# The second layer of batches one and two as seven block products, in a written order

## The chip, the cores and the metric

One core of a Trainium2 chip runs the whole program. The metric is the device time of one execution in microseconds; it is told as the median of the runs. Data lies in HBM; tiles of 128 partitions lie in SBUF; TensorE multiplies from SBUF into PSUM banks; VectorE, ScalarE and GpSimd work on the tiles; SyncE issues all DMA here.

## What is computed

```
scores = scale * q @ k.T               # batch 4, heads 12, seq 448, head_dim 64
scores = where(causal mask, -1e9, scores - max)
attn   = exp(scores) / sum
x      = (attn @ v) as [1792 tokens, 768]
gate   = 1 / (1 + exp(-(x @ w_gate)))  # w_gate, w_val: 768 x 1536
out    = (gate * (x @ w_val)) @ w_out  # w_out: 1536 x 768
```

All inputs are float32. The weights come as 64-bit words and are turned into float32 on the chip.

## The kernel before

Everything is kept transposed: features lie on partitions, the 448 tokens of a batch on the free axis. A float32 product is made of three products of a reduced type, fp32r: each operand is split into a high part (a ScalarE cast) and a low part (the operand minus its high part, on VectorE or GpSimd), and TensorE adds high x high, high x low and low x high into one bank. Such a triple is one operation of the plan, with the cost 0.608. One product has 128 x 128 weights and 448 columns.

Attention runs over 24 pairs of heads, six to a batch. For a pair: `load`, `wscore` (TensorE, line 394), `softmax` (line 417 on VectorE, 424 on ScalarE, scaling on GpSimd at line 445), `shift` (a transpose by VectorE, line 460, and a trip of the tile to DRAM and back, `pd`, `pt`), `wpv` (TensorE, line 488), `features`. The first six pairs take another path (`score`, `trans`, `pv`).

The perceptron runs in units. `unit_items(0)` and `unit_items(1)` handle batches one and two singly. The first layer (`f_in`) has 12 blocks jj, each with a gate and a value group of six triples over k; line 622 takes the gate, line 628 the gated product, lines 630 and 631 split it. The second layer (`f_out`) has six output blocks m of 12 triples each. `weight(p)` gets the weights of a group: for unit 0 it loads 64-bit words into a part of the tile `room` (768 KB), makes float32 of them (lines 570, 572, 574), keeps a copy in DRAM (`wdram`, line 577) and splits (lines 582, 584); for unit 1 it fetches the copy. Batches three and four are handled together by `pair_items` (line 814 on TensorE): each layer as seven products of half-size blocks with sums of blocks before and after, instead of eight. `pair_inputs` makes its sums and parts of the inputs, `mix` sums of weights, `out_inputs` those of the second layer's inputs.

The order is made in two steps. The bottom of the kernel lists all operations with due times: the units' triples in sequence, the attention steps of batches two to four spread over them by a pacing line (`TURN`, `SPREAD`). Then `Plan.order` simulates the engines with costs and due times (with hand-given shifts, `NUDGE`) and gives out the instructions in that order; each engine, and SyncE's DMA queue, works through its own list in order. Tiles of one tag share a ring of `BUFS[tag]` buffers, so an operation that writes a new tile waits for the users of the tile that many places back. `lock=True` marks VectorE operations that the simulation keeps apart from GpSimd's.

## Time and profile before

| what | value |
|---|---|
| median of 3 runs | 620.17 us (619.71 to 620.87) |
| span of the profiled execution | 617.8 us (the page lists no other time for it) |
| instructions | 11857 |
| TensorE busy | 606.7 us, 98% |
| VectorE, ScalarE, GpSimd busy | 442.5, 334.0, 306.3 us |
| DMA | 153.35 MB, mean 248 GB/s |

Busy time of an engine counts overlapping instructions once. The mean of a group is the length of one instruction by itself, with its overlap. The stages of the span: opening to some 40 us, first layer of batch one to 152.7, its second layer to 221, batch two to 382, batches three and four after that.

### The profile page before, as it was taken

What the parts mean: (1) busy time and instruction counts of PE and PEld (TensorE: products, weight loads), DVE (VectorE), ACT (ScalarE), POOL (GpSimd) and SP (SyncE); (2) the same over time, 40 slices, a digit from 0 to 9 for tenths busy, and PEclk for the clock granted to TensorE, in tenths of its full rate; (3) what the DMA queues carried; (4) which work ended last, traced back from release to release, by engine and by line L of the source; (5) the groups of instructions that cost most, each with busy time, mean ns of one, the idle gap of its engine ahead of it and who ended that gap; (6) DMA issues with size and microseconds to landing.
All of it is one profiled execution on the core that took longest, in us unless ns stands there. A gap on an engine that the chain in (4) does not pass through costs nothing.

```text
span 617.8 us, 11857 instructions
## 1 busy us (share of the span) xinstructions
PE 606.7 (98%) x4182; PEld 532.1 (86%) x4182; DVE 442.5 (72%) x1048; ACT 334.0 (54%) x754; POOL 306.3 (50%) x350
## 2 busy tenths in 40 slices
PE   6999999999989999999999999999999999999997
PEld 4578888898988888888888899999999989999996
DVE  5988999888856555455558856588746469999852
ACT  7997666666445655554657645443343443556420
POOL 4750434441300775877757766666746665501200
PEclk9999999999999999999999999999999999999999
DMA  8699999999999999888877896765433213534321
GB/s 292 198 305 343 367 375 384 319 407 364 349 380 337 360 333 335 285 305 288 298 276 254 291 324 222 271 230 178 153 103 103 77 53 102 161 119 149 104 76 59
DMA packets 54492, 153.35 MB, mean 248 GB/s; under 512 B 6048, under 2 KB 12704, under 8 KB 52128
## 3 DMA queue, kind: packets, MB, share of 16 engines
q1 hardware_dynamic: 54432, 152.59, 70.1%
q8 instruction: 33, 0.54, 0.3%
q14 instruction: 27, 0.22, 0.1%
HBM read 109.31 MB, written 43.25 MB: 247 GB/s over the span
## 4 chain that ended last, share of the span: by engine, by line
PE 89%; DMA 5%; DVE 3%; issue 1%; POOL 0%; ACT 0%; SPq 0%; DVEq 0%; ACTq 0%
PE m L601 38%; PE m L814 20%; PE s L814 11%; PE t L814 7%; PE m L488 5%; PE s L394 4%; PE t L394 2%; DMA room<-in_wp_dram 2%; DMA pd<-tb 1%; DVE sm L417 1%; PE t L320 1%; DMA wdram<-wr 1%; DMA vr<-in_vt_dram 1%; DVE pt L331 1%; PE m L344 0%
## 5 line engine op out<-in xcount | busy, mean ns | idle before, releaser
L768 POOL TENSOR_TENSOR wl<-room,wh 128x384 fp32r<-128x384 f32 x84 | 97.9, 1188 | 56.9 <-ACT wh L767 54.3
L445 POOL TENSOR_SCALAR sm<-sm,r 128x128 f32<-128x128 f32 (+3 forms) x165 | 91.1, 575 | 60.1 <-DVE r L435 37.6
L601 PE MATMUL m<-xh,wh 128*128 128x448 f32 x288 | 107.2, 372 | 0.0
L601 PE MATMUL m<-xh,wl 128*128 128x448 f32 x288 | 105.3, 366 | 0.0
L601 PE MATMUL m<-xl,wh 128*128 128x448 f32 x288 | 105.3, 365 | 0.0
L424 ACT ACTIVATE sm<-sm,mn 128x128 f32<-128x128 f32 (+3 forms) x168 | 87.7, 526 | 12.9 <-DVE mn L417 12.1
L584 POOL TENSOR_TENSOR wl<-wr,wh 128x768 fp32r<-128x768 f32 x38 | 70.8, 1880 | 29.4 <-ACT wh L582 29.3
L582 ACT CAST wh<-wr 128x768 fp32r<-128x768 f32 x72 | 59.4, 830 | 30.6 <-DVE wr L574 14.4
L767 ACT CAST wh<-room 128x384 fp32r<-128x384 f32 x84 | 39.7, 511 | 60.3 <-PE s L814 19.0
L601 PEld LDWEIGHTS m<-xh,wh 128*128 128x128 f32 x288 | 54.1, 188 | 6.5 <-issue 1.3
L601 PEld LDWEIGHTS m<-xh,wl 128*128 128x128 f32 x288 | 54.1, 188 | 4.5
L601 PEld LDWEIGHTS m<-xl,wh 128*128 128x128 f32 x288 | 54.1, 188 | 4.2
L417 DVE CUSTOM_DVE_ANT_0 sm<-s,mask 128x128 f32<-128x128 f32 (+3 forms) x108 | 42.7, 408 | 17.2 <-PE s L394 17.0
L601 PE MATMUL m<-gh,wh 128*128 128x448 f32 x144 | 53.3, 370 | 0.0
L601 PE MATMUL m<-gh,wl 128*128 128x448 f32 x144 | 52.6, 365 | 0.0
L601 PE MATMUL m<-gl,wh 128*128 128x448 f32 x144 | 52.6, 365 | 0.0
L631 POOL TENSOR_TENSOR gl<-gt,gh 128x448 fp32r<-128x448 f32 x24 | 29.0, 1212 | 41.6 <-ACT gh L630 41.6
L814 PE MATMUL m<-pt,wh 128*128 128x448 f32 x150 | 44.7, 366 | 0.0
L460 DVE STREAM_TRANSPOSE room<-sm 128x384 f32<-128x384 f32 (+2 forms) x84 | 36.0, 452 | 9.3 <-POOL sm L445 8.7
L394 PE MATMUL s<-raw 64*64 64x128 f32 (+3 forms) x432 | 36.9, 392 | 4.3 <-DMA raw<-in_qkt_dram 2.9
L584 DVE TENSOR_TENSOR wl<-wr,wh 128x768 fp32r<-128x768 f32 x34 | 33.4, 981 | 10.5 <-ACT wh L582 10.4
L488 PEld LDWEIGHTS m<-pt,vr 128*64 128x64 f32 x720 | 33.5, 137 | 7.8 <-issue 6.5
(177 smaller groups left out, 1378.3 us busy)
## 6 DMA issues: line engine op xcount, KB each, us to landing
room<-in_wp_dram SPq DMA_DIRECT2D x36, 768.0 KB, 7.5
pt<-pd SPq DMA_DIRECT2D x72, 256.0 KB, 5.4
wr<-wdram SPq DMA_DIRECT2D x45, 384.0 KB, 4.1
room<-wdram SPq DMA_DIRECT2D x45, 384.0 KB, 3.5
wdram<-wr SPq DMA_DIRECT2D x36, 384.0 KB, 7.5
pd<-room SPq DMA_DIRECT2D x12, 1024.0 KB, 4.6
raw<-in_qkt_dram SPq DMA_DIRECT2D x23, 448.0 KB, 5.5
vr<-in_vt_dram SPq DMA_DIRECT2D x24, 256.0 KB, 4.7
```

The source lines that it names most:

```text
L394: nc.tensor.matmul(out=sp[z].t[c:c + 64, o:o + ne], lhsT=q, rhs=k)
L417: plan.op("DVE", dve(n), lambda z=z, i=i, sp=sp, sm=sm, n=n, o=o, f=f, lo=lo, to=to, first=first: nc.vector.tensor_tensor_reduce(out=sm.t[ ...
L424: plan.op("ACT", act(ne, 0, 1) + 0.09, lambda z=z, sm=sm, i=i, ne=ne, off=off: nc.scalar.activation(out=sm.t[:, off:off + ne], in_=sm.t[:, ...
L445: plan.op("PL", 0.24 + w / 1200, lambda sm=sm, e=e, o=o, w=w, z=z: nc.gpsimd.tensor_scalar(out=sm.t[:, o:o + w], in0=sm.t[:, o:o + w], sca ...
L460: plan.op("DVE", dve(128 * c) + 0.03, lambda sm=sm, i=i, o=o, c=c, at=at: nc.vector.transpose(out=tv()[:, :, at:at + 32 * c].rearrange("p ...
L488: nc.tensor.matmul(out=vp.t[64 * z:64 * z + 64, i * WQ:i * WQ + rows(i)], lhsT=v.t[:, c, z], rhs=src, start=(c == 0), stop=(c == i))
L582: plan.op("ACT", act(768), lambda: nc.scalar.copy(hi_.t, t.t), [(t,)], [(hi_,)])
L584: plan.op(eng, cost, lambda: at.tensor_tensor(out=lo_.t, in0=t.t, in1=hi_.t.bitcast(F32), op=ALU.subtract), [(t,), (hi_,)], [(lo_,)], lock ...
L601: nc.tensor.matmul(out=ps.t[:, :S], lhsT=a.t[:, k, :], rhs=b.t if isinstance(b, Buf) else b(), start=(first and z == 0), stop=(last and z ...
L767: plan.op("ACT", act(w), lambda: nc.scalar.copy(f(hi_.t), x()), [(src, at)], [(hi_, e)])
L768: plan.op("PL", 0.97, lambda: nc.gpsimd.tensor_tensor(out=f(lo_.t), in0=x(), in1=f(hi_.t).bitcast(F32), op=ALU.subtract), [(src, at), (hi_ ...
L814: nc.tensor.matmul(out=ps.t[:, :S], lhsT=a.t[:, kw, :], rhs=b.at, start=bool(first and z == 0), stop=bool(last and z == 2), skip_group_che ...
```

## The change

The second layers of batches one and two no longer run singly. After both first layers `first_out` computes them together as seven block products (`FIRST` gives their order), the blocks being halves of the features (rows of `w_out` and halves of its columns) and the two batches. A block product has three output blocks of six triples. Its inputs are sums and differences of gated blocks (`inputs`), split just before use; its weights are blocks of `w_out` or sums of them (`out_weights`), which are converted from the 64-bit words when they are needed, six of the twelve in the first layer of batch two (`early`). Two sets of buffers hold the split inputs; inputs 0 to 3 have a buffer in each set, inputs 4 and 5 have one for both. Partial sums are kept in `tb` and `oa`. The gated blocks are no longer split when they are made.

The conversion works in place. The attention steps of batches three and four are paced over 1.87 first layers from the same start (0.95). Transposes of pairs 12 to 17 go through `tb` (one buffer) instead of `room`. Buffers change (`BUFS`); the program is built with `dynamic_dma_scratch_size=512`.

The simulation that made the order is gone: `TABLE` lists all operations by number in the order in which they are given out. An operation may have a second engine (`other`): low parts VectorE or GpSimd, some copies out of PSUM ScalarE or VectorE, the scaling of the softmax GpSimd or ScalarE. The 234 numbers in `OTHER` take it.

```diff
+LATE = 18
 PAIR = 2
-TURN, SPREAD = 0.95, 1.0
+TURN, SPREAD = 0.95, 0.97
 ORDER = "1256743"
+FIRST = "1267345"
+TWICE = 4
 AHEAD = 3
 EARLY = 2
 WC = 512
 EV = (1, 3)
-BUFS = dict(w64=3, wd=2, wr=3, ws=3, sm=4, raw=3, pt=2, gt=5, vr=2, st=4, tb=1)
-LAT, LOOK, SLACK = 0.04, 0.06, 0.2
+BUFS = dict(w64=3, wd=3, wr=3, ws=3, sm=4, raw=3, pt=2, gt=2, vr=2, st=4, tb=1, wt=1)
...
+TABLE = """
+    2 7 342 8 0 9 1 10 4 41 5 42 6 3 262 81 11 43 13 254 14 12 15 83 16 21 17 18 19 34 23 20 22 124 25 35 24 36 44
...
+"""
+OTHER = {int(x) for x in """
+    28 29 80 106 107 140 148 155 226 234 237 248 252 284 309 310 313 331 375 376 382 389 403 417 456 457 458 459 505
...
+""".split()}
...
+        o.alt = other and (other[0], other[1], other[3])
+        if len(self.ops) in OTHER:
+            eng, cost, fn, lock = other
...
+        order = [int(x) for x in TABLE.split()]
+        place = {n: i for i, n in enumerate(order)}
+        assert sorted(order) == list(range(len(self.ops)))
+        assert all(place[q.n] < place[o.n] for o in self.ops for q in (*o.preds, *o.after))
+        return [self.ops[n] for n in order]
...
-        tb = part(4 * WC, n % 2) if j["b"] >= PAIR else new("tb", [128, PTW], F32)
+        tb = part(4 * WC, n % 2) if n >= LATE else new("tb", [128, PTW], F32)
...
+    def low(out, x, hi, n, reads, writes, vector):
+        both = [(eng, c, lambda at=at: at.tensor_tensor(out=out(), in0=x(), in1=hi().bitcast(F32), op=ALU.subtract), True)
+                for eng, c, at in (("DVE", 0.08 + n / 960, nc.vector), ("PL", 0.06 + n / 430, nc.gpsimd))]
+        mine, other = both if vector else both[::-1]
+        plan.op(*mine[:3], reads, writes, lock=True, other=other)
+    def convert(p, tag, reads=()):
+        t = new(tag, [128, KD, 128], F32, BUFS[tag])
+        q = part(2 * DM, p % BUFS["w64"])
+        words = lambda: q.t.bitcast(I32).rearrange("p (n t) -> p n t", t=2)
+        lo, hi = (lambda: words()[:, :, 0]), (lambda: words()[:, :, 1])
+        f = lambda: t.t.rearrange("p k m -> p (k m)")
+        ri = lambda: f().bitcast(I32)
+        n = KD * 128
+        o = plan.op("SP", dma(128 * n * 8), lambda: nc.sync.dma_start(
+            out=q.t.bitcast(I32), in_=wp[p]), [], [(q,)], extra=4.2)
+        if p >= EARLY:
+            plan.behind(o, pairs[min(HP - 2, 1 + p)]["r"].ops[0])
+        plan.op("ACT", act(n) + 0.1, lambda: nc.scalar.activation(
+            out=f(), in_=hi().bitcast(F32), func=ACTF.Prelu, scale=REBIAS, alpha=SIGN), [(q,)], [(t,)])
+        plan.op("DVE", 0.47, lambda: nc.vector.tensor_single_scalar(
+            out=ri(), in_=ri(), scalar=3, op=ALU.logical_shift_left), [], [(t,)], lock=True)
+        plan.op("DVE", 0.87, lambda: nc.vector.scalar_tensor_tensor(
+            out=ri(), in0=lo(), scalar=29, in1=ri(), op0=ALU.logical_shift_right, op1=ALU.bitwise_or),
+            [(q,)], [(t,)], lock=True)
+        return t
+    def keep(t, d):
+        plan.op("SP", dma(128 * KD * 128 * 4), lambda: nc.sync.dma_start(out=d.t, in_=t.t), [(t,)], [(d,)], extra=4.2)
+    def fetched(d, tag="wr"):
+        t = new(tag, [128, KD, 128], F32, BUFS[tag])
+        plan.op("SP", dma(128 * KD * 128 * 4), lambda: nc.sync.dma_start(out=t.t, in_=d.t), [(d,)], [(t,)], extra=4.2)
+        return t
+    def split(t, vector):
         hi_ = new("wh", [128, KD, 128], F32R, BUFS["ws"])
         lo_ = new("wl", [128, KD, 128], F32R, BUFS["ws"])
         plan.op("ACT", act(768), lambda: nc.scalar.copy(hi_.t, t.t), [(t,)], [(hi_,)])
+        low(lambda: lo_.t, lambda: t.t, lambda: hi_.t, 768, [(t,), (hi_,)], [(lo_,)], vector)
         return hi_, lo_
 
+    def weight(p, u):
+        if u:
+            return split(fetched(wdram[p]), False)
+        t = convert(p, ("wr", "wd")[p % 2])
+        keep(t, wdram[p])
+        return split(t, p >= EARLY)
+    def out_weights(p, forms):
+        at = lambda mm, half: 2 * KF + 2 * mm + half
+        def piece(mm, half, tag, early=False):
+            if early or half and mm < KH:
+                forms["early", mm, half] = t = convert(at(mm, half), "wd")
+            elif ("early", mm, half) in forms:
+                return fetched(wdram[at(mm, half)], tag)
+            else:
+                t = convert(at(mm, half), tag)
+            keep(t, wdram[at(mm, half)])
+            return t
+        def mix(out, a, b, op):
+            plan.op("DVE", 0.88, lambda: nc.vector.tensor_tensor(
+                out=out.t, in0=a.t, in1=b.t, op=op), [(a,), (b,)], [(out,)], lock=True)
+        for m in range(KH):
+            f = lambda q: forms[q, m]
+            if p is None:
+                for half in range(2):
+                    piece(KH + m, half, "wd", True)
+            elif p == "1":
+                forms["1", m] = piece(m, 0, "wr")
+            elif p == "2":
+                forms["2", m] = piece(m, 1, "wd")
+            elif p == "6":
+                forms["7", m] = piece(KH + m, 0, "wd")
+                t = piece(KH + m, 1, "wt")
+                mix(f("7"), f("1"), f("7"), ALU.subtract)
+                mix(f("1"), t, f("7"), ALU.subtract)
+                forms["6", m] = f("1")
+            elif p == "3":
+                forms["3", m] = t = fetched(wdram[at(m, 1)], "wd")
+                mix(t, t, f("6"), ALU.subtract)
+            elif p == "4":
+                forms["4", m] = fetched(wdram[at(KH + m, 1)], "wr")
+            elif p == "5":
+                t = fetched(wdram[at(KH + m, 0)], "wd")
+                mix(t, t, f("4"), ALU.add)
+                forms["5", m] = t
...
+    def first_out():
+        items, st, u2, u3, forms = [], {}, {}, {}, {}
+        def inputs(e, some):
+            p = FIRST[e]
+            if e == 0 and TWICE not in some:
+                T["sets"] = [[cells(f"ob{i}", 1, F32R, 1)[0] for i in range(2 * TWICE)]]
+            elif e == 0:
+                apart = T["sets"][0]
+                own = [c for k in range(KD) for t in ("xh", "xl") for c in cells(f"{t}{k}", 1, F32R, 2)]
+                T["sets"] = [apart + own[2 * TWICE:], own]
+                acc = cells("tb", 5, F32, BUFS["tb"]) + cells("oa", 1, F32, 1)
+                for i in range(KH):
+                    u2[i], u3[i] = acc[i], acc[KH + i]
+            here = T["sets"][e % 2]
+            for j in some:
+                g11, g21, g12, g22 = (first.get((y, j, z)) for z in range(2) for y in range(2))
+                hi, lo = here[2 * j:2 * j + 2]
+                raw = Cell(new("gt", [128, S], F32, BUFS["gt"])) if p in "67" else None
+                x = {"1": g11, "2": g21, "5": g11, "6": raw, "7": raw, "4": g21, "3": g22}[p]
+                if p == "6":
+                    add(g11, g12, g11, ALU.subtract)
+                if p in "67":
+                    add(raw, g22, {"6": g11, "7": g12}[p], ALU.subtract)
+                if p == "6":
+                    add(g21, g21, raw, ALU.subtract)
+                halves(x, hi, lo)
+                T["f" + p, j] = hi, lo
+        def f_out(e, m, k, due):
+            p = FIRST[e]
+            if m == 0 and k == 0:
+                if e == 0:
+                    out_weights(p, forms)
+                    inputs(0, range(TWICE, KD))
+                if e < 6:
+                    inputs(e + 1, range(TWICE))
+            if k == 0:
+                st["w"] = split(forms[p, m], True)
+                if m == KH - 1 and e < 6:
+                    out_weights(FIRST[e + 1], forms)
+                st["ps"] = new("m", [128, 512], F32, 3, PSUM)
+            ps = st["ps"]
+            triple(ps, st["w"], k, T["f" + p, k], k == 0, k == KD - 1, due)
+            if m == KH - 1 and k >= TWICE and e < 6:
+                inputs(e + 1, (k,))
+            if k < KD - 1:
+                return
+            a, c = u2[m], u3[m]
+            def plus(out, x):
+                plan.op("DVE", dve(S), lambda: nc.vector.scalar_tensor_tensor(
+                    out=out.at, in0=ps.t[:, :S], scalar=0.5, in1=x.at, op0=ALU.mult, op1=ALU.add), [(ps,), x.ref], [out.ref])
+            def done(x, row, u):
+                o = Cell(new("gt", [128, S], F32, BUFS["gt"]))
+                plus(o, x)
+                plan.op("SP", dma(128 * S * 4), lambda: nc.sync.dma_start(
+                    out=out[row * 128:(row + 1) * 128, u * S:(u + 1) * S], in_=o.at), [o.ref], [], due + 10.0, extra=4.2)
+            if p == "1":
+                plan.op("ACT", act(S, 1), lambda: nc.scalar.activation(
+                    out=a.at, in_=ps.t[:, :S], func=ACTF.Copy, scale=0.5), [(ps,)], [a.ref])
+            elif p == "2":
+                done(a, m, 0)
+            elif p == "6":
+                plus(a, a)
+            elif p == "7":
+                plus(c, a)
+            elif p == "3":
+                plus(a, a)
+            elif p == "4":
+                done(c, KH + m, 0)
+            elif p == "5":
+                done(c, KH + m, 1)
+                done(a, m, 1)
+        for e in range(7):
+            for m in range(KH):
+                    items.append((cost, lambda due, e=e, m=m, k=k: f_out(e, m, k, due)))
+        return items, (lambda: inputs(0, range(TWICE)), lambda: out_weights(None, forms))
...
-                T[p, i] = cells(f"xh{k}", 1, F32R, 2) + cells(f"xl{k}", 1, F32R, 2)
+                T[p, i] = T["sets"][1][2 * k:2 * k + 2]
...
-    mlp = unit_items(0) + unit_items(1)
-    half = sum(c for c, _ in mlp) / 2
+    out_items, early = first_out()
+    mlp = unit_items(0) + unit_items(1, early) + out_items
+    half = cost * 2 * KF * KD
...
-    for seq, wide, lo, hi in ((range(HP, WIDE), False, 0.0, 0.03), (range(WIDE, 2 * HP), True, 0.0, TURN), (last, True, TURN, 1 + SPREAD)):
+    for seq, wide, lo, hi in ((range(HP, WIDE), False, 0.0, 0.03), (range(WIDE, 2 * HP), True, 0.0, TURN), (last, True, TURN, 1 + SPREAD * 15 / 8)):
...
-            if ia == len(att):
-                pair_inputs()
+    pair_inputs()
```

## Rows read from the trace of the kernel before

**Rows 1.** Part 1 of the page: busy time, share of the span, instructions.
```profile
PE 606.7 (98%) x4182; PEld 532.1 (86%) x4182; DVE 442.5 (72%) x1048; ACT 334.0 (54%) x754; POOL 306.3 (50%) x350
```

**Rows 2.** Windows at the kernel's stages: busy us per engine (instructions), clock, DMA share, GB/s.
```profile
40.00:152.70 112.70, 112.70 (x858) 98.11 (x857) 103.07 (x253) 76.48 (x164) 39.16 (x55) 1.00 0.98 360
152.70:222.00 69.30, 67.43 (x449) 59.97 (x451) 44.94 (x104) 36.95 (x72) 23.36 (x32) 1.00 0.98 359
222.00:322.00 100.00, 100.00 (x908) 86.00 (x897) 53.46 (x222) 53.94 (x148) 70.78 (x86) 1.00 0.85 300
507.00:617.80 110.80, 107.17 (x525) 98.13 (x523) 85.16 (x123) 46.82 (x82) 28.11 (x23) 1.00 0.33 107
```

**Rows 3.** Waits of TensorE after the opening: total us, times, longest us.
```profile
PE m L488 <- DMA vr<-in_vt_dram: 1.9, 1, 1.9
...
PE t L814 <- ACT xh L841: 0.6, 1, 0.6
```

**Rows 4.** Part 5 of the page, TensorE: count, busy us, mean ns, idle before.
```profile
L601 PE MATMUL m<-gh,wh 128*128 128x448 f32 x144 | 53.3, 370 | 0.0
```

**Rows 5.** The chain in order of time: start us, us, what.
```profile
570.89 31.73 PE m L814 x156
...
603.84 10.35 PE s L814 x51
```

**Rows 6.** Timeline of TensorE, 152 to 181 us: start us, us, work.
```profile
152.68 0.36 PE L601 MATMUL m<-gh,wh 128*128 128x448 f32 x1
...
160.07 2.00 PE L488 MATMUL m<-pt,vr 128*64 128x128 f32 x40
...
178.72 2.00 PE L488 MATMUL m<-pt,vr 128*64 128x128 f32 x40 [1.87 <-DMA vr<-in_vt_dram]
```

**Rows 7.** DMA issues up to 178.7 us: tiles, count, KB each, us to landing.
```profile
room<-in_wp_dram SPq DMA_DIRECT2D x34, 768.0 KB, 7.4
wdram<-wr SPq DMA_DIRECT2D x31, 384.0 KB, 7.5
```

**Rows 8.** Groups by line, the other engines.
```profile
L584 POOL TENSOR_TENSOR wl<-wr,wh 128x768 fp32r<-128x768 f32 x38 | 70.8, 1880 | 29.4 <-ACT wh L582 29.3
...
L574 DVE SCALAR_TENSOR_TENSOR wr<-room,wr 128x768 int32<-128x768 int32 x36 | 35.0, 971 | 0.6
...
L572 DVE TENSOR_SCALAR wr<-wd 128x768 int32<-128x768 int32 x36 | 21.8, 606 | 7.0 <-DMA wdram<-wr 4.4 <-ACT wd L570 2.4
...
L755 DVE TENSOR_TENSOR wl<-room,wh 128x768 fp32r<-128x768 f32 x21 | 20.3, 973 | 0.7 <-ACT wh L753 0.5
...
L683 DVE TENSOR_TENSOR xl<-m,xh 128x448 f32<-128x448 f32 x30 | 18.7, 622 | 29.4 <-PE m L814 29.1
...
L683 DVE TENSOR_TENSOR xl<-xl,xh 128x448 f32<-128x448 f32 x3 | 3.2, 1071 | 0.0
...
L688 ACT CAST pt<-gh 128x448 fp32r<-128x448 f32 x10 | 5.4, 569 | 2.5 <-PE m L814 1.4 <-DVE gh L683 1.2
```

**Rows 9.** Windows 222 to 382 us (ten head pairs): lines 417, 460, 445 alone.
```profile
222.00:382.00 160.00, 29.23 (x160) 1.00 0.83 290
...
222.00:382.00 160.00, 29.95 (x70) 1.00 0.83 290
...
222.00:382.00 160.00, 36.12 (x70) 1.00 0.83 290
```

**Rows 10.** Timeline of VectorE and GpSimd, 404 to 410 us.
```profile
404.57 2.71 POOL L768 TENSOR_TENSOR wl<-room,wh 128x384 fp32r<-128x384 f32 x2 [0.58 <-ACT wh L767]
...
404.67 1.73 DVE L777 TENSOR_TENSOR wd<-wr,wd 128x768 f32<-128x768 f32 x1
...
406.32 0.61 DVE L683 TENSOR_TENSOR xl<-s,xl 128x448 f32<-128x448 f32 x1
...
406.86 1.24 DVE L777 TENSOR_TENSOR wr<-wr 128x768 f32<-128x768 f32 x1
...
408.13 0.96 DVE L777 TENSOR_TENSOR wr<-wd,wr 128x768 f32<-128x768 f32 x1
```

**Rows 11.** DMA issues, 152.7 to 222 us: output writes.
```profile
out_dram<-gt SPq DMA_DIRECT2D x6, 224.0 KB, 6.0
```

More of the change, by code (lines that the diff above doesn't have):

```diff
@@ L1 @@
-import heapq
 from contextlib import ExitStack
@@ L94 @@
 class Op:
[L95 removed]
+    __slots__ = ("eng", "cost", "fn", "due", "preds", "succs", "make", "left", "ready", "n", "extra", "after", "then", "lock", "alt")
 class Plan:
```

236 lines of the change are left out of this document (63 added, 173 removed), and 149 rows, old and new, of tables (NUDGE, OTHER, TABLE).

## The prediction

> **What bounds the kernel now.** I read the page's head first: TensorE is busy 98% of a span of 617.8 us [rows 1]. Then the span cut at the kernel's own stages: TensorE is all but full in every one of them, at a granted clock of 1.00, while VectorE runs from about half to 91% and the DMA engines stand at 97 to 98% in the first two stages [rows 2]. Then TensorE's waits: after the opening there are two, of 1.9 and 0.6 us [rows 3]. So the time is TensorE's list of products plus about 11.1 us in which it has none (617.8 - 606.7): those 1.9 and 0.6 us, 3.6 us after the last product (107.17 of 110.8 us in the last stage [rows 2]), and so some 5 us in the opening. Any product taken off the list shortens the span, as long as nothing else then arrives late.
>
> What one product is worth must not be read from its mean duration. The group says 370 ns [rows 4], but products overlap: in the chain of waits 156 of them follow one another in 31.73 us and 51 in 10.35 us, 0.203 us each [rows 5]. The sum goes by 0.203.
>
> **The change, part by part.**
>
> *Products.* The second layer of batches one and two takes 12 blocks x 6 outputs x 3 products x 2 batches = 432 products before, and 7 block products x 3 x 6 x 3 = 378 after. 54 fewer x 0.203 = 11.0 us. Weight loads are hidden behind products before and after. By the mean duration it would be 20.0 us; the rows of the chain exclude that.
>
> *The stall at 177 us.* The first layer of batch one ends at 152.68 us; batch two's fifth and sixth head pairs reach TensorE at 160.07 and 178.72 us, the last one 1.87 us late, behind its DMA [rows 6]. Until now the second layer of batch one covers this. After the change batch two's first layer follows at once and needs all six pairs; with the two remaining bursts of 2.0 us it could start at some 156.7 us. The last pair must therefore come some 22 us earlier. What is freed: up to 178.7 us, 34 converted-weight loads and 31 write-backs were issued, where the first layer needs 24 of each [rows 7]. Ten loads of 768 KB and seven writes of 384 KB are 10.6 MB, and at the 360 GB/s of that stage [rows 2] 29.5 us of DMA. VectorE is freed as well: ten conversions at 0.606 + 0.971 us and about as many low parts at 0.973 us [rows 8] are some 25 us. 29.5 and 25 against 22: it fits, with little over. I let the stall of 1.9 us go and charge nothing new; kept at worst by a transfer that is not moved ahead, it costs up to 22 us.
>
> *Added work in the new second layer.* It lasts 126 triples x 3 x 0.203 = 76.7 us on TensorE. By the pacing line (0.95 + 1.87 x i/14 first layers) steps 8 to 13 of the last 14 attention steps fall into it: four scores and six value products, taken at 2.0 us each [rows 6], 20 us. So 97 us. VectorE's own list there, at the durations of [rows 8]: 38 low parts of inputs x 0.62 (4 more lie in the stage ahead), 24 input sums x 0.62, 12 weight sums x 0.97, 6 conversions x 1.58, 21 weight low parts x 0.97, 21 output sums x 0.62: 23.6 + 14.9 + 11.6 + 9.5 + 20.4 + 13.0 = 93. Neighbours overlap by some 0.08 us (that of 404.67 us ends at 406.40, the next began at 406.32 [rows 10]), so 128 operations fill about 83 us. The attention adds four softmaxes at 2.9 us and five transposes at 3.0 us (29.23 and 29.95 us for ten pairs [rows 9]), 26.7 us. Sum 110 us for 97 us. The change can take this in two ways. It flips the engine of 234 operations: moving 13 us of low parts costs GpSimd 1.9 times as much (1.880 for 0.973 us), 25 us on top of four pairs' scaling of 3.6 us each [rows 8, 9], 40 us of 97. And the stage before has room: per pair 5.9 us of VectorE for 8 softmaxes and 7 transposes (44 us), 12 gatings, 6 early conversions and 4 low parts make 64 us, where TensorE has 144 x 0.609 + 14 x 2.0 = 116 us; the inputs and weights of the first two block products, some 20 us, depend on batch one alone and can go there. So I let VectorE keep up, at the edge.
>
> GpSimd and VectorE also hinder each other: beside two of GpSimd's low parts the weight sum of 768 columns took 1.73 us and the next one 1.24, and 0.96 us where GpSimd was idle as it began [rows 10]; a sum of 448 columns from two SBUF tiles took 1.071 us on the mean of three, one with an operand in PSUM 0.622 [rows 8]. The Trainium skill, "SBUF — State Buffer" (SBUF: two separate sides), says that an operation of VectorE with two SBUF inputs and one of GpSimd that reads SBUF hold a port pair one after the other, for the whole instruction. The lengthening in [rows 10] agrees.
>
> *The seams.* The change gives the low and high parts of inputs 4 and 5 one buffer for all block products, so those of the next product can only be written once the current one has used them, and are wanted four triples (2.4 us) plus one later. A ScalarE copy and a VectorE subtraction, 0.57 + 0.62 us [rows 8] and their hand-overs, fit if both engines are free at once. There are six seams. Bounds: nothing, as all but one block product of batches three and four begin now without a wait, that one 0.6 us [rows 3]; and 1.5 us each, 9 us in all, if the engine that is asked is two operations behind. Batches three and four have inputs ready two products ahead, so it will not be nothing: I take 0.5 each, 3 us.
>
> *What I cost at nothing.* The conversion in place (no separate tile) has the same operations. A ScalarE copy and a GpSimd low part for each of 24 gated blocks go; neither engine sets the end. Second-layer weights: 12 loads and write-backs as before, and 15 fetches for 12, 1.2 MB more, hidden in stages at 300 GB/s or less [rows 2]. Output tiles fall from five to two: the products with an output write one per block of 18 products (3.66 us), the last writes two. In the crowded stretch a write landed after 6.0 us [rows 11]; at that, VectorE would be held up some 2 us in each of the last three blocks, when little else hangs on it. The opening and the tail are left as they are: 5 and 3.6 us.
>
> *The sum.* 617.8 - 11.0 - 1.9 + 3.0 = 607.9 us of span. The median of the runs is 620.17, 2.4 us above the profiled span; the page gives no time of its own for the profiled execution. So 610.3 us.
>
> **The rivals.**
>
> *Part of the gain is given back at the seams and at the start of batch two* (6 to 8 us instead of 3): 613.5 to 618.9 us. For it: the slack of 3 to 7 us found at 156 us, and a VectorE at the edge; six conversions of the new second layer also share the staging room with the transposes of the last six pairs. Against: in batches three and four a VectorE at 77% over the whole stage [rows 2] left TensorE without a wait of any length after 504 us [rows 3].
>
> *VectorE and GpSimd become the bound of the new second layer, and it is slower.* The place is the 97 us after batch two's first layer. If nothing is done ahead and sums and low parts beside GpSimd run at their hindered lengths (12 weight sums at the mean of 1.73, 1.24 and 0.96 us, 24 input sums at 1.07), the 110 us become about 125; moving 15 us of low parts away brings VectorE to 110 us, and the GpSimd operations so added hinder it further, so that a second move gains nothing: 13 to 14 us late. Span 617.8 - 11.0 - 1.9 + 3.0 + 14 = 621.9, time 624.3 us. It decides from about 10 us of lateness on. For it: [rows 10]. Against: 41 us of it can go to stages with room.
> By the rule of the Trainium skill named above, taken strictly, the operations with two SBUF inputs and all of GpSimd's form one line: by an estimate 68 us of VectorE's (62 operations at 0.54 us, 39 at 0.89) with GpSimd's 14 before any move, 96 after a move of 14 us, about the length of the stage; so by the rule too the time would be 610 us, but with no slack, and any further move to GpSimd would be late one for one, which is inside this rival's chance.
>
> *Batch two's last pair is not moved ahead.* Up to 22 us late at 156 us: 617.8 - 11.0 - 1.9 + 22 + 3 + 2.4 = 632 us. Against: the 29.5 us of freed DMA lie ahead of it in the same queue.
>
> *The written order also takes out idle time in the opening or the tail*: below 604.5 us at best (8.6 us are there, some of them the first load and the last write).
>
> **How the numbers follow.** A measurement of this kernel tells about 0.2% from no change, 618.9 to 621.4 us. My forecast, 604.5 to 613.5 us: 0.60. Still better: 0.04. Part given back, up to 618.9: 0.16. Within 0.2%: 0.05. Slower, by VectorE and GpSimd 0.11, by the late pair 0.04: 0.15. So faster 0.80, same 0.05, slower 0.15. Leaving out some 0.04 below and 0.16 above, the range is 604.5 to 620.8 us; the likeliest case alone is 604.5 to 613.5.
>
> **What would show it.** TensorE with 4128 products and about 596 us busy; products still 0.203 us apart. At the start of batch two's first layer no wait, and its value products before it. In the new second layer VectorE over 90% busy and TensorE's waits at block-product seams, under a microsecond each, released by VectorE's or ScalarE's input halves. I am wrong if TensorE waits there for weight low parts or sums for more than 10 us together, if a DMA releases a long wait near 156 us, or if the time falls by far more than 11 us, which would mean that the order itself was worth more than the products.

## The result and the profile after

The changed kernel takes 625.54 us (median of 5 runs, 622.46 to 627.62) beside 620.17 us for the one before: ratio 1.0078, 95% interval 1.0049 to 1.0107. It is 0.8% slower. I had forecast 610.3 us and given 0.80 to "faster".

The profiled execution took 627.62 us, the longest of the five, with a span of 625.7. Part 1 of its page (engine, busy us, share, instructions), beside [rows 1]:

```profile
PE 602.5 (96%) x4128; PEld 524.0 (84%) x4128; DVE 503.3 (80%) x1195; ACT 370.8 (59%) x849; POOL 167.0 (27%) x186
```

The 54 products are gone (4128 for 4182). But TensorE's busy time fell by 4.2 us instead of 11.0, and its idle time rose from 11.1 to 23.2 us: 12.1 - 4.2 = 7.9 us, which is the longer span. In the groups (count, busy, mean ns, idle before) the products now have idle time before them, where [rows 4] had none; two of a triple's three lines:

```profile
L786 PE MATMUL m<-xh,wh 128*128 128x448 f32 x366 | 137.2, 375 | 5.7 <-ACT gt L810 2.6
L786 PE MATMUL m<-xl,wh 128*128 128x448 f32 x366 | 134.4, 367 | 2.9 <-DVE xl L653 2.9
```

In the chain of waits the products still follow at 21.95 / 108 = 0.203 us, as in [rows 5]:

```profile
544.38 21.95 PE m L1022 x108
```

Windows by stage (busy us of PE, PEld, DVE, ACT, POOL with instructions, clock, DMA share, GB/s), beside [rows 2]:

```profile
40.00:152.40 112.40, 106.71 (x887) 88.42 (x886) 92.32 (x263) 79.40 (x187) 32.26 (x37) 0.98 0.96 344
...
280.00:340.00 60.00, 54.27 (x414) 45.67 (x413) 59.29 (x141) 43.13 (x101) 21.56 (x18) 0.97 0.79 272
...
510.00:625.70 115.70, 110.97 (x544) 101.70 (x542) 85.00 (x139) 49.58 (x90) 23.87 (x17) 1.00 0.34 110
```
```profile
222.00:280.00 58.00, 57.83 (x475) 50.60 (x472) 41.10 (x129) 37.91 (x97) 11.72 (x18) 1.00 0.93 334
```

Two stages lost most of the time. Batch one's first layer, in which TensorE had not been idle at all, now has 5.7 us of idle time. In the new second layer 5.7 of the 60 us from 280 on are missing, and there VectorE is busy 59.29 of 60 us, although it had stood idle for 16.9 of the 58 us before. Another 1.8 us is one wait at 392 us, and the time behind the last product is 0.9 us longer. TensorE's waits (total us, times, longest) answer to [rows 3]:

```profile
PE m L786 <- DVE xl L653: 2.9, 2, 1.6
PE m L786 <- ACT gt L810: 2.6, 2, 1.9
PE m L786 <- ACT wh L691: 2.1, 1, 2.1
PE s L1022 <- DVE wl L653: 1.8, 1, 1.8
```

Lines of its timeline, with the wait in brackets. The first is batch two's last pair, which stands at 178.72 in [rows 6]; the others lie in the new second layer:

```profile
152.37 2.00 PE L584 MATMUL m<-pt,vr 128*64 128x128 f32 x40 [0.74 <-DMA pt<-pd]
```
```profile
289.59 0.47 PE L786 MATMUL m<-xl,wh 128*128 128x448 f32 x1 [1.32 <-DVE xl L653]
...
299.67 0.48 PE L786 MATMUL m<-xh,wh 128*128 128x448 f32 x1 [2.11 <-ACT wh L691]
...
301.08 0.74 PE L786 MATMUL m<-xh,wl 128*128 128x448 f32 x1 [0.73 <-DVE wl L653]
```

The product at 301.08 takes 0.74 us, twice the 0.370 us of [rows 4]. Windows of TensorE alone (us, busy, granted clock, DMA share, GB/s) say why:

```profile
61.70:65.10 3.40, 3.03 (x9) 0.50 1.03 357
...
300.70:304.10 3.40, 3.02 (x25) 0.50 0.91 255
304.10:307.50 3.40, 3.40 (x56) 1.00 1.01 399
392.80:396.20 3.40, 3.40 (x11) 0.50 0.54 202
```

Three times, each behind waits of 1.75 to 2.84 us together (1.86; 2.11 and 0.73; 1.75), the granted clock stood at 0.50, the 1.2 GHz level, for a stretch of 3.4 us. At half speed such a stretch costs at most 1.7 us, so up to 5.1 in all. The trace of before has no such stretch ahead of its last products. The Trainium skill, "TensorE: Matmul & The Clock Gate" (HAM oscillation — how this bites in real kernels), names this second price of a wait, slower products after it. The rows here agree that it is paid; the last section says where they do not.

The timelines of VectorE and of GpSimd at the place where the 1.32 us wait arises show the same hindrance as [rows 10], but larger:

```profile
284.39 0.61 DVE L653 TENSOR_TENSOR xl<-gh,xh 128x448 fp32r<-128x448 f32 x1
284.93 1.90 DVE L653 TENSOR_TENSOR wl<-wr,wh 128x768 fp32r<-128x768 f32 x1
286.74 2.25 DVE L766 TENSOR_TENSOR gh<-gh,gt 128x448 f32<-128x448 f32 x1
288.92 0.61 DVE L653 TENSOR_TENSOR xl<-gh,xh 128x448 fp32r<-128x448 f32 x1
```
```profile
284.71 1.29 POOL L653 TENSOR_TENSOR xl<-gh,xh 128x448 fp32r<-128x448 f32 x1 [2.60 <-ACT xh L771]
285.97 2.55 POOL L653 TENSOR_TENSOR wl<-wr,wh 128x768 fp32r<-128x768 f32 x1
303.01 0.15 POOL L552 MEMSET room<- 128x64 f32 x1 [14.49 <-DVE wd L675]
```

A VectorE sum of 0.61 us takes 2.25 us: it ends when GpSimd's subtraction has ended (288.52) and 0.47 us more have passed. The `xl` behind it is what TensorE waits for until 289.59. GpSimd then stands idle for 14.49 us, waiting for VectorE.

The groups that answer to [rows 8], where the operation took 1880 ns on GpSimd and 973 ns on VectorE, show it on the mean: 1950 and 1066 ns. Writes landed sooner than in [rows 11], after a median of 2.0 us in the new second layer:

```profile
L653 POOL TENSOR_TENSOR wl<-wr,wh 128x768 fp32r<-128x768 f32 x17 | 33.1, 1950 | 55.9 <-ACT wh L691 48.5
...
L653 DVE TENSOR_TENSOR wl<-wr,wh 128x768 fp32r<-128x768 f32 x28 | 29.8, 1066 | 12.9 <-ACT wh L691 12.9
```
```profile
out_dram<-gt SPq DMA_DIRECT2D x10, 224.0 KB, 2.0
```

### The profile page after: what moved, and what is told of

It reads as the page before. It is cut to its first block, busy times and chain, and to the rows that moved or that the text cites. A ratio compares the mean times of both kernels' runs of the same rounds, so it can differ in the third digit from the quotient of the medians.

```text
span 625.7 us, 11784 instructions
## 1 busy us (share of the span) xinstructions
PE 602.5 (96%) x4128; PEld 524.0 (84%) x4128; DVE 503.3 (80%) x1195; ACT 370.8 (59%) x849; POOL 167.0 (27%) x186
## 4 chain that ended last, share of the span: by engine, by line
PE 68%; DVE 12%; DMA 9%; ACT 6%; issue 2%; POOL 2%; SPq 0%; DVEq 0%; ACTq 0%; POOLq 0%
PE m L786 23%; PE m L1022 19%; PE s L1022 10%; PE t L1022 7%; DMA room<-in_wp_dram 5%; PE m L584 3%; ACT sm L523 3%; PE s L493 3%; DVE sm L516 2%; DVE wl L653 2%; POOL sm L539 1%; PE t L493 1%; DMA pd<-tb 1%; DVE wr L675 1%; DMA pd<-room 1%
## 5 line engine op out<-in xcount | busy, mean ns | idle before, releaser
L786 PE MATMUL m<-xh,wh 128*128 128x448 f32 x366 | 137.2, 375 | 5.7 <-ACT gt L810 2.6
L523 ACT ACTIVATE sm<-sm,mn 128x256 f32<-128x256 f32 (+3 forms) x168 | 87.6, 523 | 31.3 <-DVE mn L516 31.1
L539 POOL TENSOR_SCALAR sm<-sm,r 128x384 f32<-128x384 f32 (+3 forms) x75 | 45.1, 619 | 104.7 <-ACT sm L523 38.5
L653 POOL TENSOR_TENSOR wl<-room,wh 128x384 fp32r<-128x384 f32 (+1 forms) x27 | 33.3, 1237 | 138.4 <-ACT wh L976 110.5
L653 DVE TENSOR_TENSOR wl<-room,wh 128x384 fp32r<-128x384 f32 (+1 forms) x78 | 54.1, 698 | 13.9 <-ACT wh L976 9.7
L542 ACT ACTIVATE sm<-sm,r 128x128 f32<-128x128 f32 (+3 forms) x93 | 43.1, 516 | 10.6 <-DVE r L534 8.1
L653 POOL TENSOR_TENSOR wl<-wr,wh 128x768 fp32r<-128x768 f32 x17 | 33.1, 1950 | 55.9 <-ACT wh L691 48.5
L556 DVE STREAM_TRANSPOSE tb<-sm 128x384 f32<-128x384 f32 (+2 forms) x84 | 33.6, 438 | 8.3 <-ACT sm L542 6.1
L653 DVE TENSOR_TENSOR wl<-wr,wh 128x768 fp32r<-128x768 f32 x28 | 29.8, 1066 | 12.9 <-ACT wh L691 12.9
L1022 PE MATMUL m<-sm,wh 128*128 128x448 f32 x126 | 36.8, 365 | 0.0
L584 PE MATMUL m<-pt,vr 128*64 128x128 f32 (+1 forms) x720 | 35.9, 255 | 0.7 <-DMA pt<-pd 0.7
```

What stands on the lines that cost most here:

```text
L523: plan.op("ACT", act(ne, 0, 1) + 0.09, lambda z=z, sm=sm, i=i, ne=ne, off=off: nc.scalar.activation(out=sm.t[:, off:off + ne], in_=sm.t[:, ...
L539: plan.op("PL", 0.24 + w / 1200, lambda sm=sm, e=e, o=o, w=w, z=z: nc.gpsimd.tensor_scalar(out=sm.t[:, o:o + w], in0=sm.t[:, o:o + w], sca ...
L542: other=("ACT", act(w) + 0.1, lambda sm=sm, e=e, o=o, w=w, z=z: nc.scalar.activation(out=sm.t[:, o:o + w], in_=sm.t[:, o:o + w], func=ACTF ...
L556: plan.op("DVE", dve(128 * c) + 0.03, lambda sm=sm, i=i, o=o, c=c, at=at: nc.vector.transpose(out=tv()[:, :, at:at + 32 * c].rearrange("p ...
L584: nc.tensor.matmul(out=vp.t[64 * z:64 * z + 64, i * WQ:i * WQ + rows(i)], lhsT=v.t[:, c, z], rhs=src, start=(c == 0), stop=(c == i))
L653: both = [(eng, c, lambda at=at: at.tensor_tensor(out=out(), in0=x(), in1=hi().bitcast(F32), op=ALU.subtract), True) for eng, c, at in ((" ...
```

## The experiments

**What a removed product is worth.** Two kernels take 54 products out of the kernel before and change nothing else: one in the second layers of batches one and two (36 of them in batch one's), the other in those of batches three and four.

```diff
-            plan.op("PE", cost, mm(st["w"], k, (gh, lambda: gl.t[:, c]), c == 0, c == KF - 1, due),
+            skip = c == 5 or (c == 4 and u == 0)
+            plan.op("PE", cost, (lambda: None) if skip else mm(st["w"], k, (gh, lambda: gl.t[:, c]), c == 0, c == KF - 1, due),
```

> The kernel before with 54 of its 432 second-layer products of batches one and two left out (the triples c = 5 of all twelve output blocks and c = 4 of batch one's six), everything else as before. Theory A (54 products are worth 11.0 us, and the changed kernel lost more than that elsewhere, in waits of TensorE and in the clock): 609.2 us, 608 to 611. Rival B (products outside the bound are worth less, because TensorE only takes up time in which it would wait anyway): 614 us or more. By the mean duration of one product it would be 600.

```diff
-        def mm(ps, w, kw, x, first, last, due, e=0):
+        def mm(ps, w, kw, x, first, last, due, e=0, skip=False):
...
-            plan.op("PE", cost, f, [(hi, e), (lo, e), xh.ref, xl.ref], [(ps,)], due)
+            plan.op("PE", cost, (lambda: None) if skip else f, [(hi, e), (lo, e), xh.ref, xl.ref], [(ps,)], due)
...
-            mm(ps, st["w"], k, T["o" + p, k], p in "165" and k == 0, k == KD - 1, due)
+            mm(ps, st["w"], k, T["o" + p, k], p in "165" and k == 0, k == KD - 1, due, skip=k == 4 and e < 6)
```

> The kernel before, less 54 products of the low parts in the second layer of batches THREE and FOUR (block k = 4 of six column tiles is left out; weights, sums and conversions all stay), where the trace of before shows no wait of TensorE longer than a few tenths. It leaves out part of the second layer's sums. Theory A (a product is worth its 0.203 us only where TensorE alone bounds; the first run took 54 out where it waited for DMA, and got 1.5 us): span falls by nearly 54 x 0.203 = 11 us, time about 609. Rival B (the products are never worth their pitch, because VectorE or DMA stand just behind TensorE everywhere): 614 or more.

Measured: 618.07 us, ratio 0.9969 (0.9952 to 0.9987), some 1.9 us: rival B. And 611.47 us, ratio 0.9882 (0.9862 to 0.9902), some 7.3 us: between theory A and rival B. In the first, TensorE's waits grew where the products went. Its window of batch one's second layer, the longest wait, and the clock behind that wait:

```profile
152.70:222.00 69.30, 64.74 (x432) 55.00 (x432) 46.19 (x111) 38.12 (x73) 25.66 (x33) 0.98 0.99 366
```
```profile
PE m L488 <- DMA vr<-in_vt_dram: 2.4, 1, 2.4
```
```profile
178.40:181.80 3.40, 3.40 (x35) 0.53 1.04 417
```

DMA stands at 0.99, and TensorE, 4.6 us idle for 1.9 before, waits for it. That is 2.7 of the 9.1 us that are missing. The half clock behind the wait took up to 1.7 more in the profiled execution, and new waits of 0.92 and 0.84 us at 357 and 370 us another 1.8; the rest is not traced. In the last second layer, where DMA stood at 0.33 [rows 2], 54 products brought four times as much, but not 11.0 us either. New waits took part of it: 1.4 us for `wl` at 575 and 582 us, and, ahead of the removed products, 1.2 us for `pt` at 376. In its profiled execution (613.74 us, the longest of the five) the stretch from the first removed product to the end is 8.9 us shorter than before.

```profile
PE m L814 <- DVE wl L755: 1.4, 2, 0.9
PE m L488 <- DMA pt<-pd: 1.2, 1, 1.2
```

So 54 x 0.203 was an upper bound; some 2 and 7 us are what two places paid.

**Is it the flips, or the written order?** One kernel keeps `TABLE` and empties `OTHER`; one gives out the order by the simulation of the kernel before (without `NUDGE`) and empties `OTHER`; one does the latter and keeps `OTHER`.

```diff
-OTHER = {int(x) for x in """
...
+OTHER = set()
```

> The changed kernel with the list of flipped engines emptied; the written order stays. Theory A (the written order has no slack: it was made for these engines and these durations): slower than the changed kernel by 10 us or more, 635 or above, since 234 operations then stand on engines the order did not count on. Rival C (the flips themselves, GpSimd's long low parts beside VectorE, cause the waits): faster, under 622.

```diff
-        order = [int(x) for x in TABLE.split()]
...
+            o = min((o for o in q if o.ready <= t + LOOK), key=lambda o: (o.due, o.n))
...
```

> The changed kernel with the order made by the simulation of the kernel before, without its hand-given shifts, and with every operation on its first engine. Theory A (waits come from the order): TensorE's idle time differs from the changed kernel's 23 us by several us either way, and its waits lie at other places. If the block products fit in a plain order, 612 to 618. Rival D (VectorE cannot do the new second layer in any order): VectorE full from about 280 to 350 us, waits there longer than the 5.7 us of the changed kernel, 626 or more.

> As the run with the simulated order, but with the 234 flipped engines kept. Theory A: the flips relieve VectorE in the new second layer (about 25 us less of it), so less idle time of TensorE there than with first engines: 3 to 6 us faster than that run. Rival C (flips hinder): slower than it.

Measured: 645.89 us (ratio 1.0430, 1.0395 to 1.0465), 662.33 (1.0678, 1.0646 to 1.0709) and 660.64 us (1.0653, 1.0623 to 1.0683). The flips are worth some 20 us within the written order, as theory A of the first run had it, and the written order some 35 against the simulation's. Neither as a whole makes the change slow; without them it would be far slower. That does not clear each single flip. The simulated order missed the 612 to 618 us of a plain order by far, but not by rival D: VectorE was busy for only 57.68 of the 70 us from 280 on. In the simulated order the flips brought 1.7 us, less than the 3 to 6 expected, and the two intervals overlap. That order waits for DMA and for late weights:

```profile
PE m L482 <- DMA pt<-pd: 12.5, 4, 5.6
PE m L684 <- ACT wh L589: 9.8, 3, 5.5
```

**VectorE in the new second layer.** The 24 input and weight sums work on 64 columns, at the same place and with the same waits.

```diff
...
-                out=out.t, in0=a.t, in1=b.t, op=op), [(a,), (b,)], [(out,)], lock=True)
+                out=h(out), in0=h(a), in1=h(b), op=op), [(a,), (b,)], [(out,)], lock=True)
...
-                    add(g11, g12, g11, ALU.subtract)
+                    add(g11, g12, g11, ALU.subtract, cut=64)
...
```

> The changed kernel, with the 24 sums over the second layer's inputs and weights (12 input blocks of the in-place chain, 12 weight sums) in batches one and two worked on 64 columns only: the instructions, their order, their waits and their engines stay, VectorE has about 17 us less to do between 222 and 340 us. It leaves out part of those sums. Theory A (in that stage VectorE is late in the written order: 5.7 us of waits from 289 to 322, and a half-clock stretch behind the 2.1 us one): those waits are gone, time falls 5 to 8 us to 617.5 to 620.5, while the waits of batch one's first layer (4.7 us before 152) stay. Rival D (the waits there come from weights, GpSimd or ScalarE, VectorE being only the last in the chain): less than 2 us.

Measured: 620.50 us, ratio 1.0017 (1.0000 to 1.0033), 0.6% or 3.8 us less than the changed kernel, and no low clock ahead of the end. By the ratio that is short of theory A's 5 to 8 us, and its word that the waits would be gone is wrong. From 280 to 340 us they shrank from 5.7 to 3.8 us, and VectorE stayed full for 19.5 of 20 us where they arise. A 64-column sum took 1.86 us there and ended just behind GpSimd's subtraction, at 285.78 and 285.70 us, so its length is not VectorE's own:

```profile
283.92 1.86 DVE L767 TENSOR_TENSOR gh<-gh,gt 128x64 f32<-128x64 f32 x1
```
```profile
283.15 2.55 POOL L653 TENSOR_TENSOR wl<-wr,wh 128x768 fp32r<-128x768 f32 x1
```

**GpSimd's subtractions beside VectorE's.** Four of them go to VectorE, in their place in the order.

```diff
+OTHER -= {1519, 1531, 1594, 1805}
```

> The changed kernel, order kept, with four of GpSimd's two-input subtractions in the new second layer (those at 277.9, 284.7, 286.0 and 319.3 us, during which VectorE's own two-input operations took 6.7 us longer than they do alone) put on VectorE in their place, where they cost it 3.2 us. Theory F (GpSimd's two-input operations hold VectorE's): VectorE gains 3.5 us there, TensorE's waits at 289 and 299 shrink by 1 us or more each and the low clock behind the second goes, 2 to 5 us faster, 620.5 to 623.5. Rival G (VectorE is simply full there, and each operation more on it makes it later): no faster than the changed kernel, 625.5 or more.

Measured: 619.45 us, ratio 0.9983 (0.9967 to 0.9999), 0.95% or 5.9 us less than the changed kernel, by four operations that cost VectorE 3.2 us. Theory F, a little beyond its range. (The lengthening that it names as 6.7 us I now read as 5.7: 2.48, 1.90, 2.25 and 2.23 us for operations of 0.96, 0.95, 0.61 and 0.61.) The same sum as above takes 0.62 us again, the subtraction itself 0.95, and the waits at 289 and 322 us are gone. Those for a weight, 2.11 and 0.73 us at 300, are now 1.22 and 0.80 at 295 and 296, and against the expectation the clock still fell behind them. The run does not separate two effects, that VectorE is no longer held and that the low parts themselves are ready sooner (0.95 for 2.55 us); the wait at 289 was for VectorE's own `xl`, behind the held sum:

```profile
286.14 0.95 DVE L652 TENSOR_TENSOR wl<-wr,wh 128x768 fp32r<-128x768 f32 x1
...
288.68 0.62 DVE L765 TENSOR_TENSOR gh<-gh,gt 128x448 f32<-128x448 f32 x1
```
```profile
PE m L785 <- ACT wh L690: 1.2, 1, 1.2
...
PE m L785 <- DVE wl L652: 0.8, 1, 0.8
```
```profile
297.60:301.00 3.40, 3.40 (x33) 0.52 1.00 310
```

**Both reliefs together** (the diffs of the last two).

> The changed kernel with both earlier edits of the new second layer: the 24 input and weight sums worked on 64 columns only (so part of those sums is left out), and the four GpSimd subtractions put on VectorE. Theory F plus A (GpSimd's hold and VectorE's load are two costs of one place, and the rest lies elsewhere): the waits from 286 to 322 fall from 5.7 to under 1 us, no low clock there, 616 to 618; what then still separates it from 609 is the waits of batch one's first layer and at 387, the tail, and products that give back less than their pitch. Rival D (the waits at 295 to 297 come from the late weights): they stay near 2 us, 619 or more.

Measured: 615.23 us, ratio 0.9937 (0.9922 to 0.9951), 1.41% or 8.7 us less than the changed kernel; the two alone add up to 9.7. Theory F plus A, a little below its range. These gains compare ratios with an interval each, so each is known to about 2 us: 8.7 can be 6.7 to 10.7, 5.9 can be 3.9 to 7.9. From 280 to 340 us TensorE is idle 0.84 us instead of 5.73, VectorE is no longer full, and no stretch has a low clock ahead of the end:

```profile
280.00:340.00 60.00, 59.16 (x484) 50.60 (x477) 54.91 (x166) 47.08 (x115) 19.71 (x19) 1.00 0.84 299
```

The traces give the same order without the medians. All four executions have done the same work of TensorE when batch two's last value product starts. From there to the end the changed kernel took 625.7 - 152.37 = 473.3 us, with short sums 618.7 - 149.09 = 469.6, with four subtractions moved 618.3 - 149.47 = 468.8, and with both 613.3 - 149.45 = 463.9.

```profile
149.45 2.00 PE L584 MATMUL m<-pt,vr 128*64 128x128 f32 x40 [0.52 <-DMA pt<-pd]
```

**ScalarE in batch one's first layer.** Two conversions go behind ready work; the list of ScalarE's operations by number:

```diff
-306 472 302 305 298 388 309 317 313 310 486 322 500
+306 302 305 298 472 388 309 317 313 310 322 486 500
```

> The changed kernel, every instruction kept, two weight conversions of ScalarE in batch one's first layer put later in its own order: the one that stood 3.2 us for its transfer until 54.99 goes behind three exponentials that were ready, the next one behind the tanh whose lateness made TensorE wait 1.86 us at 61.1. Theory A (a written order that lets an instruction wait for DMA ahead of ready work, and a wait of about 2 us with 3.4 us at half clock behind it): the wait at 61 is gone or under 0.5 us and so is the low clock at 61.7, 2 to 4 us faster, 621.5 to 623.5. Rival E (DMA is the bound of that stage, at 0.94 to 0.99 busy, so the wait only moves to the next weights): less than 1 us, and a wait of like size further on before 152.

Measured: 623.68 us, ratio 1.0077 (1.0062 to 1.0091): by the ratio no gain. The tanh came at 57.86 us instead of 60.53 and the low clock at 61.7 is gone, but TensorE now waits 1.3 us at 60.4 for the next low part and another 1.1 us at 80.4. The wait moves on, as rival E said; its reason, that DMA is the bound, does not hold, as the next experiment shows. The low clock is no gain of this edit either. The three kernels above have the changed kernel's list up to 213 us, and none has it there: the conversion that waited 3.20 us for its load until 54.99 waited 1.34, 1.84 and 0.19 us in their executions. They reach the last value product at 149.09 to 149.47 us, this kernel at 149.72.

```profile
PE m L785 <- DVE gh L813: 1.3, 2, 1.1
PE m L785 <- POOL wl L652: 1.3, 1, 1.3
```

**New orders.** Three kernels keep all operations; `TABLE` and the choice in `OTHER` are written anew.

```diff
 TABLE = """
...
 OTHER = {int(x) for x in """
...
```

> The changed kernel with its order written anew, and with another choice of VectorE or GpSimd for the low parts (some 180 of them), the operations themselves all kept. The order places what is late in the three stages with waits (ScalarE's conversions behind ready work, VectorE's sums of the new second layer earlier, GpSimd's two-input subtractions where VectorE isn't at two-input sums). Theory A (what was lost is the written order's, not the operations'): TensorE's waits fall from 15.7 us to 6 or less, the low-clock stretches go, 608 to 613, so faster than both kernels. Rival D (VectorE and DMA can't serve seven products in those stages in any order): waits stay above 12 us, 621 or more.

> The changed kernel written in yet another order, begun from that of the run with ScalarE's two conversions moved, with less GpSimd work beside VectorE's two-input operations, and moved so that each instruction that follows a transfer has the room by which transfers were late in four earlier traces. All operations kept. Theory A (the lost time is the written order's): waits below 10 us, no low clock, 612 to 618, so faster than the kernel before. Rival D (seven products in the new second layer can't be served, whatever the order): waits of 12 us or more again and 621 or above, as the run with the first new order.

> As the other new order, but begun from the first new order (the one that came out at 628.5 us) and mended for late transfers in the same way. All operations kept. Theory A: 612 to 618. Rival D: 621 or above. If this one stays above 621 and the other does not, the first new order's greater share of GpSimd work is what it suffers from.

Measured: 628.52 us (ratio 1.0151, 1.0136 to 1.0165), 630.46 (1.0161, 1.0130 to 1.0192) and 624.14 us (1.0068, 1.0046 to 1.0090). All miss theory A by 6 us and more, and reach the times of rival D. The first has GpSimd busy 234.2 us instead of 167.0 and waits of 2.3 us on GpSimd's `xl`, 3.3 us on a ScalarE copy; TensorE is idle 7.0 of the 60 us from 280 on. The other two have no less on GpSimd (247.2 and 245.4 us), so they do not settle how much of the loss is GpSimd's share; and three bad orders do not show that no order is good. They do show that VectorE is full in each: 58.66, 59.09 and 59.52 of the 60 us. None placed VectorE's work earlier: from 222 to 280 us it was busy for 36.4, 35.9 and 39.4 us, less than the 41.1 of the changed kernel. What that would bring stays untested.

```profile
PE 603.1 (96%) x4128; PEld 520.6 (83%) x4128; DVE 504.3 (80%) x1166; ACT 361.1 (58%) x828; POOL 234.2 (37%) x236
```
```profile
280.00:340.00 60.00, 53.00 (x404) 44.16 (x404) 58.66 (x134) 36.65 (x86) 28.86 (x25) 0.97 0.71 249
```

The third settles another point. In batch one's first layer it left TensorE idle for 0.85 us with DMA at 0.99, and it reached the last value product at 147.71 us without a wait, after as many products:

```profile
40.00:152.40 112.40, 111.55 (x951) 93.59 (x944) 96.22 (x274) 85.39 (x201) 51.58 (x54) 1.00 0.99 365
```
```profile
147.71 2.00 PE L582 MATMUL m<-pt,vr 128*64 128x128 f32 x40
```

So DMA at that share does not force the waits of this layer; another order and choice of engines avoids them. It lost its time from 280 us on.

**Ten subtractions moved, then a conversion chain earlier.** The four operations and six more that held VectorE go to VectorE, with ScalarE's two conversions moved as above; then, in a second kernel, a weight conversion at 290 us goes ahead of softmax work and sums.

```diff
+OTHER -= {1519, 1531, 1594, 1805, 417, 565, 593, 1640, 2074, 2082}
```

> The changed kernel, all operations kept, with the four GpSimd subtractions and six more that held VectorE by 0.8 to 1.4 us each (three in batch one's first layer, one at 303, two at 372 and 381) put on VectorE, and ScalarE's two conversions in batch one placed later. Theory F: as the run with four (619.45 us) and 1 to 3 us better, 616.5 to 618.5, clearly faster than the kernel before. Rival G (VectorE is full, only the four were worth it): 619 to 622.

```diff
 ScalarE
-1563 1559 1575 1596 1601 1634 1606 1641 1629
+1563 1596 1559 1601 1575 1641 1634 1606 1629
 VectorE
-1529 1632 1565 1576 1633 1597 1566 1598 1602 1577 1603 1642
+1529 1597 1598 1632 1602 1603 1565 1576 1633 1566 1577 1642
```

> As the first best version, with the conversion chain of two weights at 290 us (whose lateness made TensorE wait 1.22 and 0.80 us at 295 and 296) ahead of three softmax exponentials and of VectorE's sums, on ScalarE and VectorE. Theory A (the order there): those 2 us and the low clock behind them go, 1 to 3 us faster than the first best version. Rival D (what is put later is then waited for): within 1 us of it, with waits of the same sum up to 325.

Measured: 618.20 us, ratio 0.9972 (0.9956 to 0.9988), and 618.59 us, ratio 0.9986 (0.9966 to 1.0007). The first is faster than both kernels, by 0.3% against the one before, and within theory F's range; its interval overlaps that of the four alone, so the six others are not shown to be worth anything. The second is not shown to be faster than the kernel before. It only turned two waits (1.21 and 0.80 us at 296 and 298) into one of 2.11 us, rival D:

```profile
295.79 0.47 PE L785 MATMUL m<-xh,wl 128*128 128x448 f32 x1 [2.11 <-DVE wl L652]
```

## Why the prediction was wrong

- *Products.* The count was right, the pitch too, but 11.0 us was taken as their worth. The runs show 1.9 us where DMA was full and 7.3 us where it was not. In the changed kernel TensorE's busy time fell by 4.2 us, to 602.5 instead of the 596 that I had named; in the run with both reliefs, which has no low clock, it fell by 606.7 - 599.4 = 7.3 us:

```profile
PE 599.4 (98%) x4128; PEld 521.0 (85%) x4128; DVE 487.4 (79%) x1199; ACT 370.4 (60%) x849; POOL 158.3 (26%) x182
```

So this term was mis-sized, by 3.7 us at the best that a run showed. Short waits are part of it, by an estimate: one product counts as 0.370 us busy and the next should follow after 0.203, so one that comes up to 0.17 us late leaves no idle time.
- *The stall at 177 us.* Right. Batch two's last pair comes at 152.37 us, 26 us earlier, with a wait of 0.74 us. The rival of a late pair is out: up to 157 us 26 loads and 23 write-backs were issued, where [rows 7] has 34 and 31 up to 178.7. But the list of batch one's first layer was rewritten with the rest, and I did not look at it because its operations stayed. DMA is as full there as before (0.96 for 0.98), and TensorE now waits for a late tanh, copies and low parts. That was idle time that no term of the sum had: 5.7 us in this execution, 3.2 to 3.5 in the three with the same list, and 0.85 in the third new order. So it is the order's and the engines', not the stage's.

```profile
room<-in_wp_dram SPq DMA_DIRECT2D x26, 768.0 KB, 7.5
...
wdram<-wr SPq DMA_DIRECT2D x12, 384.0 KB, 5.2
wdram<-wd SPq DMA_DIRECT2D x11, 384.0 KB, 7.0
```

- *Added work in the new second layer.* This step failed: "So I let VectorE keep up, at the edge", at nothing. VectorE was as full as I had said, but two things in the step were wrong. The work that "can go there" to the stage with room did not go: VectorE was idle 16.9 us from 222 to 280 and full from 280 on. That this made it late is argued; no run moved the work. And I let low parts move to GpSimd at GpSimd's price alone, although [rows 10] and the rule named beside them said that they hold VectorE. This is shown: four such operations cost 5.9 us, and with VectorE's load eased as well 8.7 us came back. The rival "VectorE and GpSimd become the bound of the new second layer" had the place and the mechanism; its 13 to 14 us were too much. That its 624.3 us lies near 625.54 is luck: the products brought less than it assumed, and batch one's first layer added waits that it did not have.
- *The rule on the port pair* (the Trainium skill, "SBUF — State Buffer", SBUF: two separate sides). The trace agrees, with 2.25 us for a sum of 0.61. My estimate by it came out at "no slack" on the mean of the stage; the waits arose from where the operations stood, not from their sum.
- *The seams.* 3.0 us charged; the two waits for low parts of inputs took 2.9 us. The size was right by chance: both go when GpSimd's operations go, so they were not the single buffer's.
- *What I cost at nothing.* Output tiles and DMA: right (VectorE waited 0.9 us for an output tile). The tail is 4.5 us instead of 3.6. The first product of the pairs' layer waited 1.8 us for a low part at 392, which no step had; it was 0.3 us in the run with ten subtractions moved, where two at 372 and 381 us had left GpSimd. But TensorE was idle for only 0.17 us from 340 to 392 in the run with both reliefs, which left those two in place, so the cause stays open.
- *The low clock* was in no step: up to 5.1 us in the profiled execution.
- *A sum.* The rival "Part of the gain is given back" is added up wrongly: 6 to 8 us instead of 3 make 613.3 to 615.3 us, not up to 618.9. The main sum does not use it.

By ratios, forecast and result are 1.0078 - 0.984 = 2.4% apart, 14.8 us. VectorE and GpSimd in the new second layer are some 8.7 of them, by the run with both reliefs. What is left is read from its profile. The span of 613.3 us is 5.4 above the 607.9 of the forecast: 3.7 in TensorE's busy time (599.4 for 595.7) and 1.7 in its idle time (13.9 for 617.8 - 11.0 - 1.9 + 3.0 - 595.7 = 12.2). Of that idle time 3.4 us lie in batch one's first layer:

```profile
40.00:152.40 112.40, 108.96 (x935) 90.94 (x936) 93.97 (x270) 82.78 (x195) 32.88 (x39) 1.00 0.97 361
```

How much of the 3.7 us are short waits, and where they lie, stays open. The run with both reliefs is 0.6% faster than before: so much the change gains once VectorE is out of the way, with the rest still paid. But it leaves out sums that the result needs; the four subtractions, which a kernel can move, bring the changed kernel to 619.45 us.

## What to carry to other kernels

Price an operation moved from VectorE to GpSimd at what VectorE loses while it runs, not at GpSimd's time: four two-input subtractions of 1.3 to 2.6 us cost this kernel some 5.9 us while GpSimd was 27% busy. When TensorE is at 98%, ask what stands just behind it in the stage where work is taken off: 54 products gave 1.9 us in one place and 7.3 us in another. The sum of a stage does not say whether its work comes in time: look at where the list places it, also in stages whose operations stay. And one profiled execution can have waits that others of the same list lack (3.20 us for a load here, 0.19 there), so look at several before an edit is credited with their going.

## What the hardware showed that I had not expected

The clock. Three waits of TensorE of some 2 us were followed by 3.4 us at 0.50 in the changed kernel, and its five runs differ along with it: 627.62 us at a mean granted clock of 0.991, 622.46 us at 0.996. Such a stretch also followed a wait of 2.42 us in the kernel with 54 products of batches one and two removed. But the length of a wait alone does not decide. The kernel before waited 1.87 us at 178.72 [rows 6] and kept its clock, and so did the kernel with late products removed, behind a wait of 2.51 us at 180.75 us:

```profile
180.70:184.10 3.40, 3.35 (x47) 1.00 1.04 419
```

The first new order fell to 0.50 behind a wait of 3.3 us at 291, and the kernel with the conversion chain earlier, behind 2.11 us, did not. The nearest pair is the same two products: waits of 1.22 and 0.80 us at 295 and 296 were followed by 0.52 with four subtractions moved, and waits of 1.21 and 0.80 us at 296 and 298 by no fall with ten. What tells these cases apart stays open.
